# PSUM banks in two pools by whether they were written in part, and one output block of the last set transposed by TensorE

## The chip, the cores and the metric

The kernel runs on one core of a Trainium2 chip. The metric is the device time of one execution in microseconds (us). Each comparison runs the kernel and the kernel before in turns on the same chip; "mean" and "median" are over the executions of one kernel in one such call.

## The reference

A layer norm, a linear attention with 32 heads, a gated MLP, and a gated residual. All inputs are bf16; the sequence has 2048 rows, D = 1024, F = 3584.

```python
phi = lambda t: where(t > 0, t + 1, exp(t)) + 1e-6
def A(x, wqkv, wo):                       # linear attention, 32 heads of 32
    q, k, v = split(x @ wqkv)
    kv  = einsum("bhsd,bhse->bhde", phi(k), v);  z = einsum("bhsd->bhd", phi(k))
    num = einsum("bhqd,bhde->bhqe", phi(q), kv)
    den = einsum("bhqd,bhd->bhq", phi(q), z) + 1e-6
    return merge(num / den) @ wo
def B(x, w_gate, w_up, w_down):
    return (silu(x @ w_gate) * (x @ w_up)) @ w_down
xn = layernorm(x)
return x + A(xn, wqkv, wo) * silu(B(xn, w_gate, w_up, w_down))
```

## The kernel before

The kernel computes its large products in sets of seven (a two-by-two block scheme with seven products in place of eight). In a set, ScalarE (ACT) or VectorE (DVE) writes a seed into a PSUM bank, and the next product of TensorE (PE) is added to it. The products on a seeded bank carry no start flag. The program has banks that were written in part, or by transposes, "re-armed" before it hands them out again: four 128-column products with the identity, the first with the start flag. What would happen without them in before was not shown.

```python
banks = deque(range(8))
def balloc():  return banks.popleft()
def bfree(b):  banks.append(b)

class Set:
    def step(self, m):
        if m == 1:
            self.a = balloc(); self.grp(1, self.a, True)       # start flag, 512 columns
            self.b = balloc()                                  # the seed: ACT writes it, no start flag later
            act([bank_r[self.a]], [bank_r[self.b]], ps[self.b][:, :], ps[self.a][:, :], ACT.Identity)
        elif m == 5:
            e = balloc(); self.grp(5, e, True)
        ...                                                    # m = 2, 6, 7, 3, 4: added without start flag

def rearm(b):
    pe_mm([ident_r, ones_r], [bank_r[b]], [(ps[b][:, 0:128], ident[:, :], ones[:, :], True, False)] +
          [(ps[b][:, 128 * q:128 * q + 128], ident[:, :], ones[:, :], False, q == 3) for q in range(1, 4)])
    bfree(b)

# start: two banks (tb) take the transposes of the first x tiles
for b in tb: rearm(b)
# key-value sums: three banks (kvb), in part written
def kv_done():
    for b in kvb: rearm(b)
def kvt(): ...; rearm(b)          # transposed key-value block
def recip(p): ...; rearm(db)      # denominators, once for each of two passes
```

`pe_mm`, `act`, `dve`, `dma` only record operations. A list scheduler then orders each engine's queue on the host, with modelled durations and a deadline for each operation.

The last step of a set (`d_set`) multiplies silu(gate) by the attention output in transposed form, transposes a 128x512 block, adds it to x, and writes 512x256 of the output when two blocks are done. Earlier sets transpose by a DMA; the very last set (pass 1, column block 3) has all four blocks transposed by TensorE into one PSUM bank:

```python
if (p, c) == (1, 3):
    defer(2, turn)        # TensorE, four 128x128 transposes, then an add by DVE from PSUM
else:
    turn_dma()            # DMA transpose SBUF to SBUF, then an add by DVE
```

Of the kernel before, what the change touches and what calls it, by code (L numbers as in the profile page):

```python
# [14 lines left out]
KB = 1024  # L15
# [204 lines left out]
def build_kernel(nc, A_x, A_wqkv, A_wo, B_w_gate, B_w_up, B_w_down, out, WINDOW=6, NWARM=14, NPE=4, LEAD=12.0):  # L220
# [12 lines left out]
    with ExitStack() as es:  # L233
# [47 lines left out]

        ps = [es.enter_context(nc.psum_tensor("ps%d" % b, [128, 512], F32)) for b in range(8)]
        bank_r = [named("bank", b) for b in range(8)]
        banks = deque(range(8))

        def balloc():
            return banks.popleft()

        def bfree(b):
            banks.append(b)  # L290

        def sem(name):
            return es.enter_context(nc.semaphore(name))
# [141 lines left out]
        for n in range(NWARM):  # L435
            b = n % 8
# [5 lines left out]
        class Set:  # L442
# [20 lines left out]

            def step(self, m):
                if m == 1:
                    self.a = balloc()
                    self.grp(1, self.a, True)
                    self.b = balloc()
                    act([bank_r[self.a]], [bank_r[self.b]], ps[self.b][:, :], ps[self.a][:, :], ACT.Identity)
                elif m == 5:  # L470
                    e = balloc()
                    self.grp(5, e, True)
                    self.s5 = s5_ring.take()
                    act([bank_r[e]], [self.s5.r], self.s5.ap(F32), ps[e][:, :], ACT.Identity)
                    bfree(e)
                elif m == 2:
                    self.grp(2, self.a, False)
                    self.out(0, 0, self.a)
                elif m == 6:
                    self.grp(6, self.b, False)  # L480
                    self.c = balloc()
                    tt([bank_r[self.b], self.s5.r], [bank_r[self.c]], ps[self.c][:, :], ps[self.b][:, :],
                       self.s5.ap(F32), ALU.add)
                elif m == 7:
                    self.grp(7, self.b, False)
                    if self.direct is not None:
                        self.direct(1, 1, self.b, self.s5)
                        return
                    d = self.dring.take()
                    tt([bank_r[self.b], self.s5.r], [d.r], d.ap(F32), ps[self.b][:, :], self.s5.ap(F32), ALU.add)  # L490
                    self.evac(1, 1, d.ap(F32), d.r, None)
                elif m == 3:
                    self.grp(3, self.c, False)
                    self.out(0, 1, self.c)
                elif m == 4:
                    self.grp(4, self.b, False)
                    self.out(1, 0, self.b)

        PAIRSEQ = ((0, 1), (0, 5), (1, 1), (0, 2), (1, 5), (0, 6), (1, 2), (1, 6), (0, 7), (0, 3), (1, 7), (0, 4),
                   (1, 3), (1, 4))  # L500
        def rearm(b):

            pe_mm([ident_r, ones_r], [bank_r[b]], [(ps[b][:, 0:128], ident[:, :], ones[:, :], True, False)] +
                  [(ps[b][:, 128 * q:128 * q + 128], ident[:, :], ones[:, :], False, q == 3) for q in range(1, 4)])
            bfree(b)



        KV0 = (12 * KB, 40 * KB)
# [57 lines left out]
        def t_tile(i):  # L567
            s = xnslot[i]
            xa = s.ap(FP16)
            ar, j, m = xt_dest(i)  # L570
            dst = ar.at(j * 8 * KB, 8 * KB, FP16).rearrange("p (k t) -> p k t", t=512)[:, :, m * 128:(m + 1) * 128]
            if i >= NPE:
                PL.op("sp", [s.r], [xt_r(i)], lambda h: h.dma_start_transpose(dst, xa), 0.08, sem=dsem("tx%d" % (i % 2)),
                      nbytes=400 * KB)
                return
            if not tb:
                tb.extend((balloc(), balloc()))
            for q, halves in enumerate(((0, 4), (4, 4)) if i == 0 else ((0, 8),)):
                k0, n = halves
                b = tb[(i + q) % 2]  # L580
                pb = ps[b][:, 0:n * 64].bitcast(FP16).rearrange("p (k t) -> p k t", t=128)
                pe_tr([s.r, ident_r], [bank_r[b]],
                      [(pb[:, k, :], xa[:, (k0 + k) * 128:(k0 + k + 1) * 128], ident[:, :]) for k in range(n)])
                xr = xt_r(i, k0, n)
                if q == 0:
                    act([bank_r[b]], [xr], dst[:, k0:k0 + n], pb, ACT.Identity)
                else:
                    dve([bank_r[b]], [xr], lambda h, k0=k0, n=n, pb=pb: h.tensor_copy(dst[:, k0:k0 + n], pb), n * 128)

        tb = []  # L590
# [25 lines left out]
            dve([src_r, b.r], [out_r], lambda h: h.scalar_tensor_tensor(  # L616
                out_ap, src, 0.0, ba, ALU.max, ALU.add), 512)

        kvb = [balloc(), balloc(), balloc()]

        def kv_ap(g):
            return ps[kvb[g // 3]][:, (g % 3) * 129:(g % 3) * 129 + 129]
# [19 lines left out]
                ACT.Identity)  # L642

        def p_piece(i, w, j):
            b = balloc()
            for k in range(2):
                ap, r = KVV[w]["R%d%d" % (k, j)]
                pe_mm([xt_r(i, 4 * k, 4), r], [bank_r[b]],
                      [(ps[b][:, :], xt_ap(i, 4 * k + q), ap[:, q, :], k + q == 0, k + q == 4) for q in range(4)])
            if w == 0:  # L650
                k_evac(i, j, ps[b][:, :], bank_r[b], "ps")
            else:
                v_evac(i, j, ps[b][:, :], bank_r[b])
            bfree(b)
# [76 lines left out]
        combos(KVV[1])  # L731
        p_piece(1, 1, 0)
        for b in tb:
            rearm(b)
        fill = deque([partial(a_tile, 0), partial(a_tile, 1)])
        stats_of = {1: x_sums(1)}
        todo = [(u, w) for u in range(1, NT // 2) for w in range(2)]
# [60 lines left out]
            dma([], [wo_r[c]], wo[c], wo_v[:, :, c * 512:(c + 1) * 512], dsem("wo%d" % c), 1024 * KB)  # L798

        def kvt():  # L800
            b = balloc()
            tv = ps[b][:, :].bitcast(FP16).rearrange("p (k t) -> p k t", t=128)
            pe_tr([KVZ_r, ident_r], [bank_r[b]], [(tv[:, g, :], KVZ[:, g, :], ident[:, :]) for g in range(NG)])
            act([bank_r[b]], [KVT_r], KVT[:, :, :], tv[:, :, :], ACT.Identity)
            rearm(b)

        mst_ring = Ring(H, 36 * KB, 1 * KB, 16)

        def m_build(g, c):
            b = balloc()  # L810
            pe_mm([KVT_r, wo_r[c]], [bank_r[b]], [(ps[b][:, :], KVT[:, g, :], wo[c][:, g, :], True, True)])
            s = mst_ring.take()
            act([bank_r[b]], [s.r], s.ap(FP16), ps[b][:, :], ACT.Identity)
            bfree(b)
            dma([s.r], [named("mscr", c)], m_scr[g * 128:(g + 1) * 128, c * 512:(c + 1) * 512], s.ap(FP16),
                dsem("mst%d" % (s.k % 4)), 128 * KB)
# [71 lines left out]
        def q_pair(p, s, stat, at=()):  # L888
            def evac(w):
                def f(i, j, ap, r, bank):  # L890
                    g = 2 * (2 * s + w) + i
                    o, orr = pq_tile(g, j)
                    phi_evac(ap, r, o, orr, "ps" if bank is not None else "sb")

                    def den_mm():
                        if p not in den:
                            den[p] = (balloc(), set())
                        db, seen = den[p]
                        mms = []
                        for q in (2 * j, 2 * j + 1):  # L900
                            mms.append((ps[db][32 * q:32 * q + 32, 0:256], Zh[:, g, :],
                                        o[:, (q % 2) * 256:(q % 2) * 256 + 256], q not in seen, False))
                            seen.add(q)
                        pe_mm([named("Zh", g), zh_r, orr], [bank_r[db]], mms)
                    defer(7, den_mm)
                return f
            run_pair(xset(stat, 0, XV[p], evac(0), d_ring), xset(stat, 1, XV[p], evac(1), d_ring), at)

        def recip(p):
# [4 lines left out]
            ea, ra, rb = e.ap(F32, 0, KB), e.ap(F32, KB, KB), e.ap(BF16, 0, KB // 2)  # L914
            er, rr = e.sub(0, KB).r, e.sub(KB, KB).r
            dve([bank_r[db]], [er], lambda h: h.tensor_scalar(ea, ps[db][:, 0:256], 16.0, EPS_PHI, ALU.mult, ALU.add), 256)
            rearm(db)
            for q in range(4):
                dve([er], [e.sub(KB + q * 256, 256).r], lambda h, q=q: h.reciprocal(
                    ra[:, q * 64:q * 64 + 64], ea[:, q * 64:q * 64 + 64]), 400)  # L920
# [129 lines left out]

        def d_set(p, c, Sx, mstat):
            gv, sv, xo = {}, {}, {}

            def fin(i, j):
                if (i, j) not in gv or (i, j) not in sv:
# [4 lines left out]
                if j not in xo:  # L1060
# [1 line left out]
                    xo[j] = (q, [])  # L1062
                    xv = q.ap().rearrange("p (m n) -> p m n", n=256)
                    dma([], [q.r], xv, xf[row:row + 512, c * 256:(c + 1) * 256].rearrange("(m p) n -> p m n", p=128),
                        dsem("xo%d" % q.k), 256 * KB)
                q, seen = xo[j]
                xv = q.ap().rearrange("p (m n) -> p m n", n=256)

# [6 lines left out]
                def turn_dma():  # L1075
                    o = pt_ring.take()
                    oa = o.ap(FP16).rearrange("p (m n) -> p m n", n=128)
                    PL.op("sp", [g.r], [o.r], lambda h: h.dma_start_transpose(oa, g.ap(FP16)), 0.08,
                          sem=dsem("tp%d" % o.k), nbytes=200 * KB)
                    tt([o.r, q.r], [q.r], xv[:, :, i * 128:i * 128 + 128], oa, xv[:, :, i * 128:i * 128 + 128], ALU.add,  # L1080
                       True)
                    done()

                def turn():
                    if not tbank:
                        tbank.append(balloc())
                    b = tbank[0]
                    pb = ps[b][:, 0:256].bitcast(FP16).rearrange("p (m n) -> p m n", n=128)
                    pe_tr([g.r, ident_r], [bank_r[b]], [(pb[:, m, :], g.ap(FP16)[:, m * 128:(m + 1) * 128], ident[:, :])
# [1 line left out]
                    tt([bank_r[b], q.r], [q.r], xv[:, :, i * 128:i * 128 + 128], pb[:, :, :],  # L1091
                       xv[:, :, i * 128:i * 128 + 128], ALU.add)
                    done()
                if (p, c) == (1, 3):
                    defer(2, turn)
                else:
                    turn_dma()
# [54 lines left out]

        def kv_done():
            for b in kvb:
                rearm(b)

        mb = deque((g, c) for g in range(NG) for c in range(2))
        for p in range(2):
# [95 lines left out]
```

## Time and profile before

748.21 us (median of 3, 747.65 to 748.36). The page of the profiled execution, its header, busy table and chain of waits:

```profile
span 746.2 us, 9376 instructions
PE 736.1 (99%) x3553; PEld 333.2 (45%) x3566; DVE 545.3 (73%) x1010; ACT 321.7 (43%) x532; POOL 17.0 (2%) x35
PE 94%; DVE 2%; ACT 2%; DMA 1%; issue 0%; SPq 0%
```

TensorE is the bound: busy for 736 of 746 us, and 94% of the chain that ended last. The timeline of PE (columns: start, length, engine, line, operation, out<-in, shapes, count; in brackets the idle time before it and what ended it) shows the re-arming groups as `ps<-ones,ident`:

```profile
22.05 0.39 PE L209 MATMUL ps<-ones,ident 128*128 128x128 f16 x4
22.27 2.75 PE L209 MATMUL ps<-H,X 128*128 128x512 bf16 x11
...
26.09 1.04 PE L209 MATMUL ps<-H,X 128*128 128x512 bf16 x4 [0.35 <-ACT ps L322]
27.03 0.40 PE L209 MATMUL ps<-ones,ident 128*128 128x128 f16 x4
27.27 0.63 PE L209 MATMUL ps<-H,TM 128*128 128x129 bf16 x8
27.74 1.02 PE L209 MATMUL ps<-H,X 128*128 128x512 bf16 x4
28.60 4.66 PE L209 MATMUL ps<-H,W 128*128 128x512 f16 x19
...
124.88 0.39 PE L209 MATMUL ps<-ones,ident 128*128 128x128 f16 x4
125.43 0.91 PE L209 MATMUL ps<-ones,ident 128*128 128x128 f16 x8 [0.16 <-DVE H L793]
126.18 0.61 PE L216 MATMUL ps<-ident,H 128*128 128x128 f16 x8
...
128.66 0.40 PE L209 MATMUL ps<-ones,ident 128*128 128x128 f16 x4
128.90 2.32 PE L209 MATMUL ps<-X,W 128*128 128x512 f16 x10
```

A group is listed as 0.39 us long, but the next instruction starts 0.22 us after it (22.05 to 22.27). Since these lines overlap, what a group costs is read from starts, not from lengths. The three groups at 124.88 hold up the line by 1.30 us, until 126.18, because they also wait for DVE to have read the banks (0.16 us on PE in the line above; their weight loads wait 0.33 and 0.29 us).

The end, from the timelines of PE, DVE and the DMA-issuing queue (SPq) of before:

```profile
742.04 1.70 SPq L332 DMA_DIRECT2D out_dram<-TM  x2
742.47 0.40 PE L216 MATMUL ps<-ident,TM 128*128 128x128 f16 x4 [0.93 <-DVE TM L329]
742.91 0.42 DVE L329 TENSOR_TENSOR TM<-ps,TM 128x512 bf16<-128x512 f16 x1 [0.49 <-PE ps L216]
```

PE waits 0.93 us for DVE before the last block's transposes. The two final output writes are issued at 742.04 and 743.36 (the two in the SPq line); the last add ends at 743.33 and the span ends 2.85 us later.

### The profile page before, as it was taken

What the parts mean: (1) busy time and instruction counts of PE and PEld (TensorE: products, weight loads), DVE (VectorE), ACT (ScalarE), POOL (GpSimd) and SP (SyncE); (2) the same over time, 40 slices, a digit from 0 to 9 for tenths busy, and PEclk for the clock granted to TensorE, in tenths of its full rate; (3) what the DMA queues carried; (4) which work ended last, traced back from release to release, by engine and by line L of the source; (5) the groups of instructions that cost most, each with busy time, mean ns of one, the idle gap of its engine ahead of it and who ended that gap; (6) DMA issues with size and microseconds to landing.
All of it is one profiled execution on the core that took longest, in us unless ns stands there. A gap on an engine that the chain in (4) does not pass through costs nothing.

```text
span 746.2 us, 9376 instructions
## 1 busy us (share of the span) xinstructions
PE 736.1 (99%) x3553; PEld 333.2 (45%) x3566; DVE 545.3 (73%) x1010; ACT 321.7 (43%) x532; POOL 17.0 (2%) x35
## 2 busy tenths in 40 slices
PE   8999999999999999999999999999999999999997
PEld 3444445434444444444444444344444444444443
DVE  6999757767798776876466687878967778657363
ACT  3677544574574343413232265546534333222231
POOL 2211100000000000000000000000000000000000
PEclk9999999999999999999999999999999999999999
DMA  9343125433773424371747633427542345346640
GB/s 306 89 113 86 29 56 165 119 100 111 213 218 97 112 57 113 99 217 52 195 99 167 174 98 85 113 71 216 168 113 69 101 125 172 99 115 167 178 104 29
DMA packets 166861, 93.55 MB, mean 125 GB/s; under 512 B 31392, under 2 KB 162720, under 8 KB 166816
## 3 DMA queue, kind: packets, MB, share of 16 engines
q1 hardware_dynamic: 166816, 92.95, 45.7%
q8 instruction: 28, 0.46, 0.3%
q14 instruction: 17, 0.14, 0.1%
HBM read 75.50 MB, written 10.62 MB: 115 GB/s over the span
## 4 chain that ended last, share of the span: by engine, by line
PE 94%; DVE 2%; ACT 2%; DMA 1%; issue 0%; SPq 0%
PE ps L209 94%; DMA W<-in_A_x_dram 1%; ACT H L322 1%; ACT TM L322 0%; SPq L332 0%; DVE TM L329 0%; ACT L322 0%; DVE W L329 0%; DVE H L793 0%; PE ps L216 0%; ACT ps L322 0%; DVE ps L329 0%; DVE H L329 0%; DVE TM L615 0%; DVE H L616 0%
## 5 line engine op out<-in xcount | busy, mean ns | idle before, releaser
L209 PE MATMUL ps<-X,W 128*128 128x512 f16 x1504 | 347.6, 379 | 1.2 <-DVE ps L329 1.2
L322 ACT ACTIVATE TM<-ps 128x512 f32<-128x512 f32 (+1 forms) x275 | 162.5, 597 | 245.5 <-PE ps L209 243.3
L209 PEld LDWEIGHTS ps<-X,W 128*128 128x128 f16 (+1 forms) x1504 | 144.8, 98 | 175.9 <-DVE ps L329 3.1
L209 PE MATMUL ps<-H,W 128*128 128x512 f16 (+1 forms) x891 | 205.2, 379 | 0.3
L329 DVE TENSOR_TENSOR W<-W 128x1024 f16<-128x1024 bf16 (+3 forms) x224 | 133.5, 628 | 14.1 <-DMA W<-in_B_w_down_dram 6.2
L209 PEld LDWEIGHTS ps<-H,W 128*128 128x128 f16 (+1 forms) x896 | 87.1, 98 | 104.6 <-DVE ps L329 0.8
L209 PE MATMUL ps<-P,W 128*128 128x512 f16 x512 | 123.0, 379 | 0.0
L329 DVE TENSOR_TENSOR ps<-ps,TM 128x512 f32<-128x512 f32 x94 | 65.5, 697 | 59.1 <-PE ps L209 58.7
L329 DVE TENSOR_TENSOR TM<-ps,TM 128x512 f32<-128x512 f32 (+1 forms) x91 | 61.4, 676 | 57.3 <-PE ps L209 56.1
L322 ACT ACTIVATE ps<-ps 128x512 f32<-128x512 f32 x94 | 55.1, 586 | 96.3 <-PE ps L209 95.5
L209 PEld LDWEIGHTS ps<-P,W 128*128 128x128 f16 (+1 forms) x512 | 49.2, 98 | 59.1 <-issue 0.2
L329 DVE TENSOR_TENSOR H<-ps,TM 128x512 f16<-128x512 f32 (+1 forms) x91 | 62.7, 690 | 15.5 <-PE ps L209 15.3
L322 ACT ACTIVATE TM<-TM 128x512 f16<-128x512 f32 (+1 forms) x61 | 37.5, 616 | 46.1 <-DVE TM L329 46.1
L329 DVE TENSOR_TENSOR H<-H 128x1024 f16<-128x1024 f16 (+2 forms) x82 | 51.5, 633 | 2.6 <-ACT H L322 1.5
L329 DVE TENSOR_TENSOR TM<-TM 128x512 f16<-128x512 f16 (+1 forms) x60 | 24.8, 421 | 20.8 <-DMA TM<-TM 15.0
L209 PE MATMUL ps<-H,X 128*128 128x512 bf16 (+1 forms) x133 | 32.5, 379 | 1.8 <-ACT X L322 0.7
L322 ACT ACTIVATE H<-ps 128x512 bf16<-128x512 f32 (+2 forms) x42 | 24.2, 614 | 15.0 <-PE ps L209 12.8
L615 DVE TENSOR_SCALAR TM<-TM 128x512 f16<-128x512 f16 x64 | 17.5, 287 | 15.4 <-ACT TM L322 15.1
L329 DVE TENSOR_TENSOR W<-H 128x1024 f16<-128x1024 f16 x38 | 25.7, 686 | 3.5 <-PE ps L209 3.3
L322 ACT ACTIVATE H<-H,zc 128x512 bf16<-128x512 bf16 x32 | 21.6, 714 | 8.8 <-DMA H<-r_scratch 8.8
L209 PE MATMUL ps<-H,P 128*128 128x512 bf16 (+1 forms) x93 | 22.8, 379 | 0.2
L209 PE MATMUL ps<-W 128*128 128x512 f16 x76 | 22.0, 379 | 0.0
(71 smaller groups left out, 295.5 us busy)
## 6 DMA issues: line engine op xcount, KB each, us to landing
W<-in_B_w_gate_dram SPq DMA_DIRECT2D x28, 512.0 KB, 4.0
W<-in_B_w_up_dram SPq DMA_DIRECT2D x28, 512.0 KB, 5.3
W<-in_B_w_down_dram SPq DMA_DIRECT2D x16, 896.0 KB, 6.7
W<-in_A_x_dram SPq DMA_DIRECT2D x16, 256.0 KB, 3.3
H<-in_A_wqkv_dram SPq DMA_DIRECT2D x8, 512.0 KB, 8.0
W<-in_A_wqkv_dram SPq DMA_DIRECT2D x8, 512.0 KB, 4.8
H<-r_scratch SPq DMA_DIRECT2D x32, 128.0 KB, 4.3
q_scratch<-H SPq DMA_DIRECT2D x8, 512.0 KB, 4.3
```

Source lines behind the costliest of these rows:

```text
L209: last = h.matmul(o, l, r, start=st, stop=sp, skip_group_check=True)
L322: return PL.op("act", reads, writes, lambda h: h.activation(o, i, func, **kw), nel(o) / 1200.0 + (0.055 if src == "ps" else 0.095))
L329: return dve(reads, writes, lambda h: h.tensor_tensor(o, a, b, op), nel(o), 1.92 if fast else 0.96)
L615: dve([e.r], [b.r], lambda h: h.tensor_scalar(ba, ea, 1.0, EPS_PHI, ALU.min, ALU.add), 512, 2.6)
```

## The change

Intent: drop the eight re-arming groups. Banks that were written in part or by transposes go to a second pool, `bare`, from which only allocations are served that begin with a full 512-column product with the start flag, or that are themselves of this kind. In the last set three blocks go to DMA transposes, with their deadline brought forward by 60 us, and only block (1,0) stays on TensorE. The diff, cut to its core:

```diff
-        def balloc():
+        bare = deque()
+        is_bare = set()
+        def balloc(fresh=False):
+            if fresh and bare:
+                b = bare.popleft(); is_bare.discard(b)
+                return b
             return banks.popleft()
+        def balloc_part():
+            b = bare.popleft() if bare else banks.popleft()
+            is_bare.add(b)
+            return b
         def bfree(b):
-            banks.append(b)
+            (bare if b in is_bare else banks).append(b)
 ...
-                    self.a = balloc()                      # set, m == 1; the same for m == 5, p_piece, m_build
+                    self.a = balloc(True)
-        def rearm(b): ...
-                tb.extend((balloc(), balloc()))            # the same for kvb, kvt, den, tbank
+                tb.extend((balloc_part(), balloc_part()))
-            rearm(b)                                       # at tb, kvb, kvt, den
+            bfree(b)
 ...
+            last = (p, c) == (1, 3)
-                        dsem("xo%d" % q.k), 256 * KB)
+                        dsem("xo%d" % q.k), 256 * KB).urgent = 60.0 * last
-                          sem=dsem("tp%d" % o.k), nbytes=200 * KB)
+                          sem=dsem("tp%d" % o.k), nbytes=200 * KB, urgent=60.0 * last)
-                if (p, c) == (1, 3):
+                if last and (i, j) == (1, 0):
                     defer(2, turn)
```

More of the change, by code (lines that the diff above doesn't have):

```diff
@@ L284, in build_kernel @@
         banks = deque(range(8))
-        def balloc():
+        bare = deque()
+        is_bare = set()
+        def balloc(fresh=False):
+            if fresh and bare:
+                b = bare.popleft()
+                is_bare.discard(b)
+                return b
             return banks.popleft()
+        def balloc_part():
+            b = bare.popleft() if bare else banks.popleft()
+            is_bare.add(b)
+            return b
         def bfree(b):
-            banks.append(b)
+            (bare if b in is_bare else banks).append(b)
         def sem(name):
@@ L470, in step @@
                 elif m == 5:
-                    e = balloc()
+                    e = balloc(True)
                     self.grp(5, e, True)
@@ L500, in build_kernel @@
                    (1, 3), (1, 4))
-        def rearm(b):
-            pe_mm([ident_r, ones_r], [bank_r[b]], [(ps[b][:, 0:128], ident[:, :], ones[:, :], True, False)] +
-                  [(ps[b][:, 128 * q:128 * q + 128], ident[:, :], ones[:, :], False, q == 3) for q in range(1, 4)])
-            bfree(b)
         KV0 = (12 * KB, 40 * KB)
@@ L617, in phi_evac @@
                 out_ap, src, 0.0, ba, ALU.max, ALU.add), 512)
-        kvb = [balloc(), balloc(), balloc()]
+        kvb = [balloc_part() for _ in range(3)]
         def kv_ap(g):
@@ L644, in p_piece @@
         def p_piece(i, w, j):
-            b = balloc()
+            b = balloc(True)
             for k in range(2):
@@ L800, in kvt @@
         def kvt():
-            b = balloc()
+            b = balloc_part()
             tv = ps[b][:, :].bitcast(FP16).rearrange("p (k t) -> p k t", t=128)
@@ L804, in kvt @@
             act([bank_r[b]], [KVT_r], KVT[:, :, :], tv[:, :, :], ACT.Identity)
-            rearm(b)
+            bfree(b)
         mst_ring = Ring(H, 36 * KB, 1 * KB, 16)
         def m_build(g, c):
-            b = balloc()
+            b = balloc(True)
             pe_mm([KVT_r, wo_r[c]], [bank_r[b]], [(ps[b][:, :], KVT[:, g, :], wo[c][:, g, :], True, True)])
@@ L896, in den_mm @@
                         if p not in den:
-                            den[p] = (balloc(), set())
+                            den[p] = (balloc_part(), set())
                         db, seen = den[p]
@@ L916, in recip @@
             dve([bank_r[db]], [er], lambda h: h.tensor_scalar(ea, ps[db][:, 0:256], 16.0, EPS_PHI, ALU.mult, ALU.add), 256)
-            rearm(db)
+            bfree(db)
             for q in range(4):
@@ L1085, in turn @@
                     if not tbank:
-                        tbank.append(balloc())
+                        tbank.append(balloc_part())
                     b = tbank[0]
@@ L1154, in kv_done @@
             for b in kvb:
-                rearm(b)
+                bfree(b)
         mb = deque((g, c) for g in range(NG) for c in range(2))
```

## The prediction

> **What bounds it.** TensorE. In the busy table it has 736.1 of 746.2 us, DVE 545.3, ACT 321.7; the granted clock is full throughout; the chain of waits is 94% matmuls. Its waits are few, so from 30 to 735 us almost only removing TensorE instructions can help.
>
> **Why the change is legal.** [...] Before, partly written banks get four 128-column identity products. After, such a bank goes to whichever allocation starts with a full 512-column product[...].
>
> **Removed.** Eight re-arming groups, 32 products. In the timeline of PE a group shifts its successor by 0.22 us (22.05 to 22.27), 0.24 (27.03 to 27.27), 1.30 for the three together (124.88 to 126.18, of which about 0.64 is waiting for the DVE readers of the key-value sums), 0.24 (128.66 to 128.90), and about 0.22 for each of the two denominator banks: 2.44 us (worked out from these). All are in line on PE.
>
> Also 12 of the 16 tail transposes: three groups at about 0.22 us. Only the first (735.46 to 735.68) is on the chain. The second lies in a stretch paced by DVE's 0.69 us subtractions, the third where PE waits for the last block.
>
> **Added, moved.** Three DMA transposes in the last set. Earlier ones show their add 2.4 to 2.5 us after issue begins (719.95 to 722.38); (1,1) and (0,1) should land by about 740 and 741.5, before the last block's product of gates at about 741.8. But the add of (0,1) now comes after that, so the first of the two final output writes starts about 0.5 us later and overlaps the last one more. I expect the tail to be neutral, -0.3 to +0.6 us. The last block keeps ACT 0.60, DVE 0.43, transposes 0.41, add 0.42, and 2.85 us to the end.
>
> **What is given back.** The instruction order shows two places where an earlier PE meets DVE. At 27 us the products on summed inputs come about 0.6 us earlier while DVE still forms the sums: perhaps 0.3 us returns. At 124 to 135 us DVE is almost solidly busy, and five more of the small denominator products now carry a DVE wait: perhaps 0.5 us of the 1.30 returns. Bank reuse elsewhere keeps several products of distance, so I expect no wait between 160 and 735 us over 0.3 us.
>
> **Sum.** 748.2 - 2.4 + 0.8 - 0.2 (first transpose group) + 0.1 = 746.5 us. Range 745.0 to 747.9. Faster by over 2%: 0.01; within 2%: 0.98; slower by over 2%: 0.01.
>
> **What would show it.** PE instructions down by 44 (32 plus 12), PE busy down by roughly 2 us; the re-arming group gone; in the window 116 to 160 us PE waits on DVE grow by 0.3 to 1 us; the chain's last 5 us after the last product unchanged in length; three more DMA transposes, with no PE waiting on them.
>
> **What would make it wrong.** A DMA transpose landing late, blocking the in-order DVE before the last block's add (up to +1 us); the two final writes competing (over +0.6 us); a bank handed on so soon that PE waits for its evacuation in each pair (then several us slower); or the freed stretches near 125 us being wholly DVE-bound (no gain there) or wholly free (745.5).

Why banks may be handed on without re-arming, no trace or run shows; shown is that the results of all runs were correct. The sum has lost no term: 748.2 - 2.4 + 0.8 - 0.2 + 0.1 = 746.5 us. That DVE is "in-order" is seen in e14 below: a statistic at the head of its queue waits 1.65 us for an x tile, the operations behind it wait with it, and PE then waits 0.72 us for one of them.

## More of the kernel before

An `urgent` value is taken off a deadline, and deadlines are handed back to all predecessors:

```python
def schedule(self):
    for o in reversed(ops):
        d = o.pecum if o.eng == "pe" else o.pecum + 30.0
        for s in o.succs:
            extra = (4.0 + o.nbytes / 200e3) if o.sem is not None else o.busy + o.lat
            d = min(d, s.dl - extra)
        o.dl = d - o.urgent
    ...   # then, engine by engine: of the operations ready by modelled time, the one due first (PE: first in the program)
```

So taking one operation away changes the modelled times of what follows, and with them the order on every engine.

## The result and the profile after

747.92 us (median of 6, 747.17 to 749.07) against 748.05 us for before in the same rounds (median of 6): ratio 0.9999, 95% interval 0.9987 to 1.0012. Ratios are the mean time of one kernel's runs over that of the other's of the same rounds, so not quite the ratio of the medians. The kernel was 1.4 us slower than predicted and lay 0.02 us above the range.

The page of after, the same three lines:

```profile
span 745.6 us, 9302 instructions
PE 734.1 (98%) x3522; PEld 330.4 (44%) x3522; DVE 541.1 (73%) x1010; ACT 321.2 (43%) x532; POOL 16.2 (2%) x35
PE 93%; DVE 2%; ACT 2%; DMA 2%; issue 0%; POOL 0%; SPq 0%
```

PE is busy for 2.0 us less, as predicted ("roughly 2 us"). Yet the span is only 0.6 us shorter, so PE idles more. The PE timeline of after, with the places that answer to those of before:

```profile
26.66 1.04 PE L209 MATMUL ps<-H,X 128*128 128x512 bf16 x4
27.53 0.63 PE L209 MATMUL ps<-H,TM 128*128 128x129 bf16 x8
28.52 1.90 PE L209 MATMUL ps<-H,W 128*128 128x512 f16 x8 [0.35 <-DVE W L344]
30.78 0.39 PE L209 MATMUL ps<-H,W 128*128 128x512 f16 x1 [0.36 <-DVE TM L625]
...
120.93 6.20 PE L209 MATMUL ps<-X,W 128*128 128x512 f16 x28
127.06 0.28 PE L209 MATMUL ps<-H,Zh 128*32 128x256 bf16 x2
...
658.62 3.19 PE L209 MATMUL ps<-H,W 128*128 128x512 f16 x14
662.28 1.04 PE L209 MATMUL ps<-X,W 128*128 128x512 f16 x4 [0.48 <-DMA W<-m_scratch]
```

Three things are to be seen. At the start, the wait of 0.35 us for ACT is gone, but two waits for DVE (0.35 and 0.36 us) have come. In the key-value stretch nothing is left where 1.30 us had been, and no wait has come for it. And at 662 us PE waits 0.48 us for a load from the scratch tensor `m_scratch`, which it did not do before. The DMA-issuing queue of after around that load:

```profile
656.44 0.37 SPq L347 DMA_DIRECT2D W<-m_scratch  x1
657.02 4.35 SPq L1088 DMA_TRANSPOSE TM<-TM  x2
```

And the same of before:

```profile
657.74 0.37 SPq L332 DMA_DIRECT2D W<-m_scratch  x1
663.13 0.37 SPq L332 DMA_DIRECT2D TM<-in_A_x_dram  x1
```

In before the load was issued at 657.74, no transfer was issued behind it until 663.13, and it landed 3.81 us after its issue. In after it took 5.80 us.

The end of after (PE, DVE and SPq):

```profile
731.57 7.79 SPq L1088 DMA_TRANSPOSE TM<-TM  x3
741.61 0.40 PE L216 MATMUL ps<-ident,TM 128*128 128x128 f16 x4 [1.15 <-DVE TM L344]
741.92 0.95 SPq L347 DMA_DIRECT2D out_dram<-TM  x2
742.04 0.42 DVE L344 TENSOR_TENSOR TM<-ps,TM 128x512 bf16<-128x512 f16 x1 [0.15 <-PE ps L216]
```

The first line is the three DMA transposes of the last set, of which PE and the last block wait for none. (The view merges them: they are issued at 731.57, 736.87 and 738.10, and each holds the queue for 1.2 to 1.3 us.) The output writes are issued at 741.92 and 742.50, only 0.58 us apart (before: 1.32). The last add ends at 742.47 and the span ends 3.15 us later, not 2.85: the second write now lands 2.64 us after its issue, not 2.29, behind the first.

The best way to add this up is to compare the start of the same weight load of PE in two traces. The table gives after minus before in us, for this profile and for those of three later repeats of the same kernel (described below):

| landmark (time in before, us) | first | e1 | e10 | e14 | mean | step of the mean |
|---|---|---|---|---|---|---|
| 11.7 (first x tiles) | +0.41 | -0.17 | +0.19 | -0.17 | +0.07 | +0.07 |
| 120.5 (before the key-value sums are read) | +0.36 | +0.34 | +0.43 | +0.67 | +0.45 | +0.38 |
| 146.5 | -1.16 | -1.18 | -1.09 | -0.85 | -1.07 | -1.52 |
| 486 (both denominators done) | -1.23 | -1.63 | -1.53 | -0.94 | -1.33 | -0.26 |
| 637 | -1.23 | -1.63 | -1.53 | -0.94 | -1.33 | 0 |
| 729 | -0.64 | -1.67 | -1.50 | -0.51 | -1.08 | +0.25 |
| end of span | -0.56 | -1.60 | -1.42 | -0.44 | -1.00 | +0.08 |

Two things follow before any experiment. The start, where 0.46 us of products were taken away, lost time as a whole. Between the first two landmarks it did so in two steps: from 34 to 47 us all four profiles stand 0.12 us ahead of before, counted from the first x tiles; then they lose 0, 0.55, 0.29 and 0.90 us (first, e1, e10, e14) between 47 and 51 us, and each 0.07 to 0.08 more by 90 us. And two of the four profiles lose 0.4 to 0.6 us near 660 us that the others do not.

### The profile page after: what moved, and what is told of

Read it like the earlier page. It is cut to its first block, busy times and chain, and to the rows that moved or that the text cites. A ratio compares the mean times of both kernels' runs of the same rounds, so it can differ in the third digit from the quotient of the medians.

```text
span 745.6 us, 9302 instructions
## 1 busy us (share of the span) xinstructions
PE 734.1 (98%) x3522; PEld 330.4 (44%) x3522; DVE 541.1 (73%) x1010; ACT 321.2 (43%) x532; POOL 16.2 (2%) x35
## 4 chain that ended last, share of the span: by engine, by line
PE 93%; DVE 2%; ACT 2%; DMA 2%; issue 0%; POOL 0%; SPq 0%
PE ps L209 93%; DMA W<-m_scratch 1%; ACT H L337 1%; ACT TM L337 1%; DMA W<-in_A_x_dram 0%; DMA H<-r_scratch 0%; DVE TM L344 0%; DVE H L344 0%; ACT L337 0%; PE ps L216 0%; ACT X L337 0%; DVE stats L555 0%; DVE W L344 0%; DVE ps L344 0%; DVE TM L625 0%
## 5 line engine op out<-in xcount | busy, mean ns | idle before, releaser
L344 DVE TENSOR_TENSOR TM<-ps,TM 128x512 f32<-128x512 f32 x88 | 60.2, 684 | 46.3 <-PE ps L209 45.9
```

The lines of the kernel that those rows point to most:

```text
L344: return dve(reads, writes, lambda h: h.tensor_tensor(o, a, b, op), nel(o), 1.92 if fast else 0.96)
```

## The experiments

There were eighteen runs of thirteen different kernels, all with correct results, with five executions each (e17: six). The theories at the outset were two (A and B in the first expectation). Theory 1: the 2.4 us are gained where predicted and lost to new waits at places that can be named. Theory 2: the gain was there, and the first verdict was scatter. Times are medians with the range; "mean" is the mean of this kernel minus the mean of before.

### Is there a gain at all? Three repeats of the changed kernel

No edit.

> The changed kernel once more, for precision and for a second profile. Theory A (the saved TensorE time is really given back, by waits that the new order makes): the mean stays within 0.7 us of the kernel before; the new profile again shows the 0.5 us wait for the m_scratch load near 662 us and the two DVE waits near 28 to 31 us. Theory B (the first verdict was scatter, such as the first x tile landing 0.8 us later in that one execution): over more rounds it is 1.2 to 2.2 us faster than before, and the wait for m_scratch is gone in this profile.

Measured: 746.93 us (746.46 to 749.19), before 748.16; mean -1.12; ratio 0.9985 (0.9972 to 0.9999). Neither theory has it whole: the size lies just below the range of B, the wait for `m_scratch` is gone in this profile, and the two waits for DVE are still there.

> The changed kernel a third time, for the size of its gain. First 0.05 us below before (6 runs), then 1.13 us below (5 runs). If the gain is real and the first verdict was scatter of DMA landings: 0.5 to 1.3 us below before. If the second was the lucky one: within 0.3 us of before.

Measured: 748.20 us (746.85 to 748.61), before 749.03; mean -1.01.

> The changed kernel a fourth time, as the yardstick of e13_after_plus on one chip. After -0.04, -1.12 and -1.01 us against before: between -1.2 and -0.5 us.

Measured: 747.45 us (747.40 to 747.82), before 748.34; mean -0.81.

So there is a gain. Over all 21 runs the mean difference, weighted by runs, is -0.71 us (-0.04, -1.12, -1.01 and -0.81 with 6, 5, 5 and 5 runs). The first was on the unlucky side, but the prediction said -1.7, and the mean is 1.0 short of that. Theory 2 explains part of the miss, not all.

### The change in parts

Pools everywhere, all four last blocks by TensorE as before:

```diff
-                        dsem("xo%d" % q.k), 256 * KB).urgent = 60.0 * last
+                        dsem("xo%d" % q.k), 256 * KB)
-                          sem=dsem("tp%d" % o.k), nbytes=200 * KB, urgent=60.0 * last)
+                          sem=dsem("tp%d" % o.k), nbytes=200 * KB)
-                if last and (i, j) == (1, 0):
+                if last:
```

> Only the two pools: no re-arming products, but all four blocks of the last set turned by TensorE and no raised urgency, as before. Theory A with the loss in the DMA order: the pools alone are 1.2 to 2.0 us faster than before (2.4 us of re-arming, less 0.4 us of waits for DVE near 28 us, less up to 0.8 us elsewhere), no wait for m_scratch. Rival (the bank hand-over itself makes the waits): 0 to 0.6 us faster.

Measured: 746.84 us (746.43 to 747.60); mean -1.41; span of the profile -1.50.

The opposite, before with the new tail alone (the same three lines of the change put into before):

> Only the tail part: re-arming kept, three of the last blocks turned by DMA with the raised urgency. Theory A with the loss in the DMA order: 0.2 to 0.9 us slower than before, with a wait of PE for a load in the second half. Rival (the tail part is neutral as predicted): within 0.3 us of before.

Measured: 748.60 us (748.15 to 748.81); mean +0.12. Its profile gains 0.38 us up to the last add and loses 0.30 us between the last add and the end, as after does. So the pools are the whole gain, and the tail gives nothing.

After without the urgency:

```diff
-                        dsem("xo%d" % q.k), 256 * KB).urgent = 60.0 * last
+                        dsem("xo%d" % q.k), 256 * KB)
-                          sem=dsem("tp%d" % o.k), nbytes=200 * KB, urgent=60.0 * last)
+                          sem=dsem("tp%d" % o.k), nbytes=200 * KB)
```

> The changed kernel with the raised urgency of the last set's DMAs taken out; everything else as changed. The urgency is passed back to everything those DMAs depend on, so it reorders the queue of the whole second half. Theory A with the loss in the DMA order: 1.0 to 2.0 us faster than before, 0.7 us faster than the changed kernel, and PE does not wait for m_scratch. Rival (the urgency is not the cause): the same time as the changed kernel within 0.3 us, or slower, because transposes come late in the tail.

Measured: 753.50 us (752.55 to 754.98); mean +5.19: slower, as the rival had it. The SPq and DVE timelines of this kernel:

```profile
741.46 1.20 SPq L1088 DMA_TRANSPOSE TM<-TM  x1
743.32 2.72 SPq L1088 DMA_TRANSPOSE TM<-TM  x2
744.40 0.42 DVE L344 TENSOR_TENSOR TM<-TM 128x512 bf16<-128x512 f16 x1 [3.85 <-DMA TM<-TM]
```

The queue reaches the last set's transposes (741.46 us) only after all products are done (739.46 us). So the urgency is necessary for this tail. It also acts elsewhere: handed back to all predecessors, it moves transposes and loads in the queue through the second half of the program.

Pools for the key-value, transposed key-value and denominator banks only; the two start banks re-armed as before; tail as before:

```diff
+        def rearm(b): ...                                  # as in before
-                tb.extend((balloc_part(), balloc_part()))
+                tb.extend((balloc(), balloc()))
-            bfree(b)                                       # for b in tb
+            rearm(b)
```

> The two pools for the six later banks only (key-value sums, their transpose, the two denominators); the two transpose banks of the start are re-armed as before; last set as before, no raised urgency. Theory C (the later removals pay in full, 1.30 + 0.24 + 0.22 + 0.22 = 2.0 us; removing the two re-armings of the start loses more to DVE waits at 28 to 62 us than their 0.46 us): 1.8 to 2.2 us faster than before, that is 0.5 to 0.8 us faster than the pools everywhere, and TensorE is within 0.1 us of the old kernel's clock at 120 us, less the scatter of the first load. Rival (the waits of the start come from any change and are worth nothing): the same as the pools everywhere, 1.3 us faster than before.

Measured: 746.66 us (746.18 to 746.88); mean -1.77. Its profile stands at +0.08 at 120.5 us (+0.09 at 11.7), at -1.44 at 146.5 and at -1.81 at the end.

And its complement, pools for the two start banks only, everything else re-armed:

> The converse: only the two transpose banks of the start go through the pool without re-arming; the six later banks are re-armed; last set as before. Theory C: no gain from eight products less, 0 to 0.5 us slower than before, with new waits of TensorE for DVE near 28 to 31 us and of DVE for an x tile near 47 us. Rival (products off TensorE pay everywhere): 0.3 to 0.5 us faster.

Measured: 748.39 us (748.37 to 749.02); mean +0.29. By the times alone this is within the scatter (ratio 1.0005, 0.9993 to 1.0018); its profile stands at -0.16 at 11.7 us and at +0.46 at 120.5 us, a loss of 0.62 us between them.

This pair places the loss. Taking away the six groups of the middle gains 1.8 us, close to the 1.98 us that their lines cost before (1.30 + 0.24 + 0.22 + 0.22). Taking away the two groups of the start, 0.46 us of products, costs 0.3 us. Leaving half of the change out is faster than the whole.

### Other tails

With the pools in the middle, and of the last set only block (0,0) by DMA, with urgency 10 (the same two lines with 10.0, and `if last and (i, j) != (0, 0)`):

> The pools for the six later banks, and in the last set only the first block turned by DMA (its four TensorE transposes were the ones on the chain), the other three by TensorE, with the urgency raised by 10 in place of 60. If the tail loses its 0.22 us to the later first output write, this keeps the early write and gains 0.2 us on the pools for the six banks alone: 2.0 to 2.4 us faster than before, time from last DVE add to end as before. Rival (the final write takes the same either way): no difference from the pools for the six banks within 0.1 us.

Measured: 746.17 us (745.73 to 747.17); mean -1.96, so 0.2 us better than e5 by the means, which is within the scatter.

With the pools in the middle, (0,0) and (1,1) by DMA, (1,0) and (0,1) by TensorE, urgency 60:

```diff
-                if last and (i, j) == (1, 0):
+                if last and (i, j) in ((1, 0), (0, 1)):
```

> The pools for the six later banks; the last set with two blocks by DMA and two by TensorE, (0,1) and (1,0), so that the first output write no longer waits for a DMA transpose behind the last gate product; urgency 60 as in the change. If the 0.30 us that the change loses between the last add and the end is the two writes running together: last add to end as before (about 2.85 us), 2.0 to 2.4 us faster than before, unless a wait for m_scratch appears. Rival: 0.3 us still lost between last add and end.

Measured: 746.04 us (745.76 to 746.42); mean -2.25; ratio 0.9971 (0.9959 to 0.9984). Here each output half has one block of either kind. The SPq timeline:

```profile
739.37 2.25 SPq L347 DMA_DIRECT2D out_dram<-TM  x2
```

The first output write is issued at 739.37, 1.9 us before the second (741.24), and the time from the last add to the end is 2.86 us again. So the tail's loss in the changed kernel is the meeting of the two writes: with one pair of blocks finished early, it is gone, and the gain of the shorter PE line stays.

### Why the start loses

In the profiles of the pools-only, start-only and changed kernels, PE waits 0.35 and 0.36 us for DVE near 28 and 30 us. In all but the first profile of the changed kernel DVE then waits 1.0 to 1.65 us for an x tile near 47 us, and PE waits up to 0.7 us for DVE again near 49.7 us. Rivals: (A) the freed PE time is worthless, since PE runs ahead to another limit; (B) the order in which banks are handed on, and so the order of instructions, is worse. To part them, the products were put back as useless work, while the bank goes to the pool of bare banks all the same (pools-only kernel otherwise):

```diff
         for b in tb:
+            pe_mm([ident_r, ones_r], [bank_r[b]], [(ps[b][:, 0:128], ident[:, :], ones[:, :], True, False)] +
+                  [(ps[b][:, 128 * q:128 * q + 128], ident[:, :], ones[:, :], False, q == 3) for q in range(1, 4)])
             bfree(b)
```

> The pools-only kernel, but the two banks of the small transposes at the start still get their re-arming products before they go to the pool of bare banks. So the order in which banks are handed on is that of the pools, while the 0.46 us of PE time at the start is not freed. Theory A (the freed time is what makes the load of an x tile and the VectorE statistics at 47 us come late or count: PE runs ahead of them, and the time is given back): same as the pools-only kernel within 0.15 us, and the PE wait behind VectorE near 49.7 us shrinks. Theory B (the order of the banks, and the instruction order that goes with it, costs the time): about 0.46 us slower than pools-only, which means about 0.9 us below before, and the 1.1 to 1.4 us VectorE wait for the x tile stays as it was.

Measured: 746.07 us (745.37 to 747.00), before 749.03; mean -2.66. Both theories fell: it was neither equal to pools-only nor 0.46 us slower, but 1.2 us faster against before (-2.66 and -1.41, on different chips). In its profile the waits at 26, 28, 30 and 49 us are all gone, and PE stands 0.65 us ahead of before at 120.5 us, though it issues every product that before issues there. So a third theory, C: not the removed time and not the banks as such, but the order that the scheduler makes of the shifted modelled times decides this stretch. It was tested on the changed kernel itself, with the same three lines as above added to it and nothing else:

> The changed kernel itself, with the two re-arming groups of the start put back as useless work (0.46 us of TensorE products; the banks still go to the pool of bare banks). The model's account, from the pools-only pair: the order that comes out with these products in place is about 1.1 us better at the start. Theory C (order decides the start): 0.7 to 1.3 us faster than the changed kernel of the same call, although it does more work. Rival (the earlier result was a lucky chip or belongs to the other tail): 0.46 us slower than the changed kernel, or the same within 0.3 us.

Measured: 746.27 us (745.46 to 746.92), against 747.45 us for the changed kernel: means 746.16 and 747.57, a difference of 1.41 us. The changed kernel becomes 1.4 us faster when 0.46 us of useless TensorE work is added. The rival, 0.46 us slower, is excluded. The PE and DVE timelines of this kernel:

```profile
26.05 1.90 PE L209 MATMUL ps<-H,X 128*128 128x512 bf16 x8
27.78 0.39 PE L209 MATMUL ps<-ones,ident 128*128 128x128 f16 x4
28.01 0.63 PE L209 MATMUL ps<-H,TM 128*128 128x129 bf16 x8
28.48 4.65 PE L209 MATMUL ps<-H,W 128*128 128x512 f16 x19
...
48.56 0.68 DVE L555 BATCH_NORM_STATS2 stats<-W 128x6 f32<-128x512 bf16 x1
49.24 1.02 PE L209 MATMUL ps<-H,X 128*128 128x512 bf16 x4
```

And the same places of the changed kernel (e14, timelines of PE, SPq and DVE), where the statistics of the x tile stand first in the DVE queue and wait:

```profile
27.93 1.90 PE L209 MATMUL ps<-H,W 128*128 128x512 f16 x8 [0.35 <-DVE W L344]
30.20 2.55 PE L209 MATMUL ps<-H,W 128*128 128x512 f16 x11 [0.37 <-DVE TM L625]
...
42.55 0.58 SPq L347 DMA_DIRECT2D W<-in_A_x_dram  x1
47.73 0.69 DVE L555 BATCH_NORM_STATS2 stats<-W 128x6 f32<-128x512 bf16 x1 [1.65 <-DMA W<-in_A_x_dram]
49.94 1.04 PE L209 MATMUL ps<-H,X 128*128 128x512 bf16 x4 [0.72 <-DVE TM L625]
```

From 11.7 to 120.5 us e13 gains 0.58 us on before (+0.47 to -0.11) and e14 loses 0.84 (-0.17 to +0.67), a difference of 1.42. Followed weight load by weight load it has two parts.

- By 47 us e13 has gained 0.57 us and e14 0.12, a difference of 0.44. In e14 the 0.46 us of products and the wait of 0.35 us for ACT are gone, but 0.35 + 0.37 us of waits for DVE have come. In e13 the re-arming products are all there, but the four products `ps<-H,X` that before issues at 27.74 come ahead of the second re-arming group, and between 20 and 47 us neither the wait for ACT nor one for DVE is left. e9 and e17, with the same products, have gained 0.54 and 0.55 us there.
- Between 47 and 51 us e14 loses 0.90 us behind the late x tile, and 0.07 more by 90 us. e13 loses none.

The traces show that the order did change. If the names of the instructions up to 120 us are aligned (without buffer numbers and without the re-arming products), at least 18 of 220 of DVE, 5 of 106 of ACT and 6 of 635 weight loads of PE stand elsewhere in the changed kernel than in before, and 41, 10 and about 20 in e13 than in the changed kernel. The order of the 40 DMA issues is that of before in the changed kernel, and one x load stands elsewhere in e13. What e13 does not part: it changes the order, PE's own time and the place of a DMA packet (below) together. No run kept the order and moved the time alone. So it is shown that the work taken away does not by itself set the time of this stretch. That the order alone sets it is argued, with the best support up to 47 us, where e9, e13 and e17 issue the products of before in another order and are 0.54 to 0.57 us ahead of it.

Is the late x tile a cause? In e14 the load was issued at 42.55 us and landed 5.16 us later. In the ten profiles of kernels with the products it was issued between 42.37 and 43.46 us, and landed 3.0 to 3.1 us later. To test it, the x loads were ranked earlier in the pools-only kernel:

```diff
-            dma([], [s.r], s.ap(), xf[i * 128:(i + 1) * 128, :], dsem("x%d" % s.k), 256 * KB).urgent = 10.0
+            dma([], [s.r], s.ap(), xf[i * 128:(i + 1) * 128, :], dsem("x%d" % s.k), 256 * KB).urgent = 15.0
```

> The pools-only kernel with the loads of the x tiles ranked earlier in the SP queue (urgency 15 in place of 10). If VectorE's wait of 1.1 to 1.4 us for an x tile near 47 us is what takes the start's gain away: that wait vanishes and the kernel is 0.3 to 0.5 us faster than pools-only, about 1.8 us below before. If the late tile is only a sign and something else paces that stretch: the same as pools-only within 0.15 us. If earlier x loads push other transfers back by as much: slower.

Measured: 746.38 us (745.61 to 747.22), before 749.03; mean -2.51. The DVE wait shrank to 0.7 us but did not vanish. Since pools-only had run on another chip, both were run again together:

> The pools-only kernel a second time, as the yardstick of e16_x15_again on one chip: 1.2 to 1.6 us below before.

Measured: 747.47 us (746.28 to 748.77), before 748.34; mean -1.04.

> The pools-only kernel with x loads ranked earlier, again, now beside pools-only on one chip. If the late x tile at 47 us is a cause: 0.3 to 1.0 us faster than pools-only. If it is only a sign, and the 2.5 us below before in the last call was the chip: within 0.2 us of pools-only.

Measured: 745.97 us (745.37 to 746.46), before 748.34; mean -2.43, 1.38 us faster than pools-only. The DVE wait was 0.6 us against 1.4. So earlier x loads help by more than was expected, but the edit reorders much else at the start too (PE now waits 0.7 us for ACT near 20 us and no longer near 28 and 30 us), and the profile of e15 holds two chance waits of PE (0.58 and 0.76 us near 201 and 210 us) that the profile of e2, the same program, does not have. At 120.5 us e15 and e16 differ by 0.92 us. This experiment agrees with the late tile as one cause of the start's loss; it does not isolate it.

The traces of the eight profiles without the start products and with the x loads ranked as before settle more. In them the first of the two x loads issued between 42 and 46 us took 3.13, 4.55, 4.56, 4.62, 4.82, 4.90, 4.93 and 5.16 us to land, and PE lost 0, 0.29, 0.29, 0.35, 0.55, 0.63, 0.67 and 0.90 us on before between 47 and 51 us. Where there is a loss, it is the time of the load less 4.26 or 4.27 us. Four of the eight are the changed kernel itself, with the same instructions in the same order. So within one order this loss is set by when the tile lands.

What goes with the late tile is to be seen in the DMA view between 40 and 48 us, forty equal slices with the busy share in tenths and the rate, first of e13, then of e14:

```profile
DMA  0000300000000089999995967999999965892000
GB/s 0 0 0 0 82 0 0 0 0 0 0 0 0 1 173 221 215 209 204 201 169 92 225 82 256 402 297 282 259 273 280 282 138 164 338 379 103 0 0 0
q8 instruction: 1, 0.02, 1.0%
```

```profile
DMA  0000000000005999997678979999920000000199
GB/s 0 0 0 0 0 0 0 0 0 0 0 0 118 230 209 215 209 198 149 117 164 123 215 297 309 291 262 118 45 82 0 0 0 1 8 10 9 22 283 288
q8 instruction: 1, 0.02, 0.7%
```

In e13 the one packet of the queue that the profile calls "instruction" (16 KB) is the lone 82 GB/s slice at 40.87 us, with nothing else in flight. In e14 it is the 82 GB/s slice at 45.86 us, in the middle of the x loads and the DMA transposes, and after it the engines deliver almost nothing for 1.6 us; single 256-byte packets then in flight took up to 2.27 us, as against mostly 0.02 us. The pattern holds in all 20 profiles that were taken: in the ten kernels with products at the start the packet begins between 40.3 and 41.5 us and the DMA transpose behind the first of the two x loads takes 3.2 to 3.5 us; in the eight profiles without them it begins between 45.3 and 46.3 us and that transpose takes 4.9 to 5.5 us; in the two with earlier x loads it begins at 43.7 and 44.3 us and the transpose takes 4.0 and 4.1 us. Within the changed kernel alone: in the first profile the tile landed at 46.26 us, the packet began at 46.27, and nothing was lost; in the other three the packet came first, and the tile landed 1.84 to 2.15 us after its begin. That is a coincidence of position in 20 of 20 profiles, not an experiment: no run moved the packet and nothing else. That it causes the stall was not shown.

The same pattern is at 656 us. Where the 16 KB packet begins at least 1.2 us after the issue of the `m_scratch` load, the load takes 4.6 to 5.8 us (nine profiles, all four of the changed kernel among them); where it begins earlier, 3.8 to 4.4 us (eleven). In the changed kernel two DMA transposes stand directly behind the load as well, and in two of its four profiles PE waited (0.48 and 0.32 us).

### Do the parts add?

Pools in the middle with the changed kernel's tail:

> Pools for the key-value, transposed key-value and denominator banks; the two start banks re-armed as before; and the changed kernel's tail. If the parts add: -1.78 (that part alone) + 0.12 (the tail alone) = about 1.7 us below before, with 0.30 us lost again between the last VectorE addition and the end. If the raised urgency of the whole second half costs more in company of the pools than alone (a wait for the m_scratch load near 660 us, as in the first profile of the changed kernel): 1.2 us below before or less.

Measured: 746.73 us (746.19 to 747.96); mean -1.82. The sum of the parts was -1.77 + 0.12 = -1.65; they add. Its profile has no wait near 660 us, and loses 0.30 us again after the last add.

The best start and the best tail together (pools everywhere, start products kept as useless work, tail of e8), and e8 again as its yardstick:

> Pools everywhere with the two useless start groups kept, and the last set with blocks (0,0) and (1,1) by DMA, (1,0) and (0,1) by TensorE. If the parts add: the start is worth -0.7 to -0.9 us against the kernel with the pools in the middle only, and the tail -0.3 to -0.5: about 0.7 to 0.9 us faster than e18_mid_two_again of this call, 2.8 to 3.2 below before. If they interfere through the reordered queue of the second half: less than 0.4 us faster than it.

Measured: 745.32 us (745.19 to 745.85, 6 runs), before 748.31; mean -2.94; ratio 0.9959 (0.9947 to 0.9972).

> The best kernel of the second call again, as yardstick: 2.0 to 2.5 us below before (measured 2.25).

Measured: 745.60 us (745.50 to 747.13); mean -2.27, as before (-2.25).

The combination is the fastest kernel, 2.9 us below before and 2.2 us below the changed kernel's mean gain of 0.71. Against e18 it gains 0.67 us by means and 0.28 by medians: the direction of the sum is confirmed, its last 0.4 us are within the scatter.

## Why the prediction was wrong, point by point

- **TensorE as the bound, and the removed time.** Right. "2.44 us" is what the lines cost before, and PE's busy time fell by 2.0 us. The denominators gave 0.22 us each wherever no chance wait fell into that stretch.
- **"At 124 to 135 us ... perhaps 0.5 us of the 1.30 returns."** Wrong, on the cautious side: the key-value stretch gained 1.52 us of 1.54 in every profile with pools there, and PE waited no more between 118 and 160 us than before. DVE was busy there, but not the last to arrive.
- **"At 27 us the products on summed inputs come about 0.6 us earlier while DVE still forms the sums: perhaps 0.3 us returns."** Right in place and size. The wait is there (0.35 us for DVE), a second one follows 2 us later (0.36 us), and a wait of 0.35 us for ACT at 26 us is gone. Of the 0.46 us, 0.34 had come back by 34 us in each of the four profiles.
- **"The instruction order shows two places where an earlier PE meets DVE."** This is the step that failed: there is a third place at the start, and the list was read from the old order. At 49.7 us PE waits for DVE, which waits for an x tile that lands late. This cost 0 to 0.90 us in the four profiles, 0.43 in the mean, and another 0.07 was lost by 90 us. So the start did not gain 0.16 us net but lost 0.38 us after the first x tiles, in the mean of four profiles: 0.84 us came back instead of 0.3. The prediction treated the order as the old one with holes; in fact the order of PE, DVE and ACT changed. Putting the products back, with the banks still pooled, gave yet another order, no late tile, and made the changed kernel 1.4 us faster.
- **"I expect the tail to be neutral, -0.3 to +0.6 us" (+0.1 in the sum, after -0.2 for the first transposes).** The transposes gave their 0.22 us, and no PE instruction waited for the three new DMA transposes. The writes met as feared and cost 0.30 us, so the sum of the tail was +0.08, not -0.1. "The chain's last 5 us unchanged in length" was wrong by that 0.30.
- **"I expect no wait between 160 and 735 us over 0.3 us."** Right for the reason given (bank reuse), wrong in fact: in two of four profiles PE waited 0.3 to 0.5 us for the `m_scratch` load. The urgency of the last set's DMAs, handed back to their predecessors, had reordered the queue far ahead of the tail. The prediction looked at the tail only. That the same wait does not come in e11 and e13, with the same tail, shows that the reordering alone does not suffice; there the load took 4.4 and 4.0 us.

Added up, as measured minus predicted, in us, with the means of the table: first x tiles and start +0.61 (+0.45 instead of -0.16; 0.43 of it at the late x tile), key-value stretch -0.48, denominators and chance waits up to 486 us +0.18, 637 to 729 us +0.25, tail +0.18. That is +0.74: the four profiles have -1.00 instead of -1.74. The 21 timed runs have -0.71; the profiles are one run each and were a little luckier than the mean. The 747.92 was in addition on the slow side of that mean.

What stays open: whether the 16 KB packet is what stalls the DMA (and so why the tile lands late), how much of the gain of e9 and e13 up to 47 us is order alone, and why the changed kernel shows the wait near 660 us in two profiles of four.

## What to carry to other kernels

In a program whose queues are ordered by a host-side scheduler, taking a TensorE instruction away is not a local edit: build it, compare the order on every engine, and price the stretch by its new waits; here 0.46 us removed at the start cost 0.4 us, because a load that nobody had on the list landed late, while 1.98 us removed in the middle gained 1.8. Split such a change by place and keep the parts that pay. At the end of a kernel, let the first output half be complete well before the second: here writes issued 0.6 us apart cost 0.3 us that writes 1.3 us apart did not.

## What the traces show of the 16 KB packets and of the transposes

- The 16 KB packets on the queue that the profile calls "instruction" begin 19.8 to 30.9 us apart and are 0.92 to 1.60 us long in before, 20.7 to 32.0 us apart and 0.88 to 2.16 us long in after. Where one falls among the x loads and transposes near 45 us, a DMA transpose lands 4.9 to 5.5 us after its issue instead of 3.2 to 3.5, and a 256 KB load up to 5.2 us instead of 3.1 (seen together in all 20 profiles, not parted by an experiment).
- One 128x128 transpose by TensorE (f16) is listed as 0.22 us, and four in a row as 0.39 to 0.40 us together, which hold up the line by 0.22 us (735.46 to 735.68 in before). The SBUF-to-SBUF DMA transpose of a 128x512 block holds the issuing queue for 1.2 us at the least and 4.7 us at the most (in after), and its data land 2.4 us after the issue at the earliest.
